# Seven block products for the output projection of the last token chunk, in a hand-scheduled two-block transformer kernel

## The chip, the cores and the metric

One core of one Trainium2 chip runs the whole program as one launch. The metric is device time in microseconds (us) of that launch. Times are quoted as the median of several runs. One further execution is recorded by the profiler; the durations in this document come from such recorded executions.

## The reference

The input x has 2048 tokens of 512 features. Two pairs of blocks follow each other, both pairs with the same weights:

```
x = x + attention(layernorm(x)) @ wo      # linear attention, 32 heads of 16 features
x = x + relu(layernorm(x) @ w1) @ w2      # hidden width 1376
```

The attention is linear: phi(t) = (t+1 if t>0 else exp(t)) + 1e-6 is applied to q and k, kv = sum over tokens of phi(k) v, and the output of a token is phi(q) kv / (phi(q) sum phi(k)). Everything is bf16 at the outside.

## The kernel before

The tokens are cut in 16 tiles of 128 and in four chunks t = 0..3 of four tiles. The code counts four layers: 0 and 2 are attentions, 1 and 3 are feed-forward layers. A name such as `2.fin12_0` is operation `fin12_0` of layer 2.

**An attention layer** makes, chunk by chunk, k and q (phi is a linear part and an exponential on ScalarE, ACT, and a minimum and maximum on VectorE, DVE), then the sum over all tokens (products `g`), and from it, in the short stage written in `bar`, a 512x512 matrix Mf: `g` is evacuated to GT (`gev`), `kv` products follow, a mask makes KVT (`kvmask`), products `m0` to `m3` with wo give Mf, evacuated one block at a time (`mev0` to `mev3`). The denominators go another way: `den` products, a logarithm and an exponential on ACT (`lnd`, `rdc`), a spreading DMA from SyncE's queue (SP, `spread`), and a DVE product that scales q (`pqs`).

The **output projection** of a tile i is then `fin`: four matmuls of 128x128 by 128x512 into one PSUM bank (for tiles 0 to 3 two calls, `fin0_0` with the first two blocks of Mf and `fin0_2` with the others). `resid` on DVE adds the bank to the residual stream xres and sums the rows, `sq` on ACT sums the squares, and for every two tiles a row of small instructions on GpSimd (POOL) and DVE (`nmean`, `msq`, `var`, `veps`, `rstd`, `nbias`) leads to the normalised tiles (`norm`) and to one DMA transpose per two tiles on SP's queue (`tr0_0`, `tr0_1`, ...), which fills Tb, the operand of the next layer.

**A feed-forward layer** computes with seven block products in place of eight (`b_h7`, `b_out`): the operands are cut in 2x2 blocks, sums of blocks are formed on DVE (`hs1` to `hs4`, `ssum`), the products `h1` to `h7` of the hidden layer run in three column groups (`_0`, `_2` of two blocks, `_4` of one), each a PE call of four or two matmuls of 256 columns. Bank BA receives h1, is copied by ACT to a second bank (`hv1`, the seed, line 700), and then goes on accumulating h6, h7 and h4; h2 is added to the copy. `hr` is the ragged rest of the hidden width.

**The order of the work** is set by a list scheduler at build time (`_list_schedule`, line 471 on). Every call of `g.add` makes one operation; its priority is its place in the order of these calls plus a whole number from the table HINTS (line 422). WINDOW is 1 for every engine, so that each engine takes its operations strictly in order of priority and waits for the next one when its inputs are not there. A second kind of hint, with "!" at the end of the key, fixes which of several engines an operation runs on (line 457). All operations that have a choice have such a hint. So the order on each engine can be read from the order of the calls and the table.

Lines that matter below: 838 `warm_fill` (eight small matmuls on zeros, `fill0`), 882 `ln_norm`, 900 the DMA transposes, 930 on `phi`, 953 all matmuls, 960 `resid`, 968 `sq`, 1147 and 1148 `gev`, 1159 `kvmask`, 1166 and 1167 `mev`, 1215 and 1217 `lnd` and `rdc`, 1227 `spread`, 1235 `pqs`, 1402 `hs`, 1797 `p2`, which chooses between `a_fin_chunk` and `f7` by the table F7 (line 650).

Of the kernel before, what the change touches and what calls it, by code (L numbers as in the profile page):

```python
# [62 lines left out]
HINTS = {"0.aqsum1": -43, "0.aqsum1!": 0, "0.aqsum2": -24, "0.aqsum2!": 0, "0.aqsum3": -126, "0.aqsum3!": 0, "0.aqsum4": 36,  # L63
         "0.aqsum4!": 0, "0.as1": -10, "0.as1_2": -24, "0.as1_2!": 0, "0.as1_3": -56, "0.as1_3!": 0, "0.as2_2": -15,
         "0.as2_2!": 0, "0.as2_3": -45, "0.as2_3!": 0, "0.as3": -6, "0.as3_2": -14, "0.as3_2!": 0, "0.as3_3": -40,
         "0.as3_3!": 0, "0.as4_2": -7, "0.as4_2!": 0, "0.as4_3": -36, "0.as4_3!": 0, "0.as_h1": -9, "0.as_h2": -6,
         "0.as_id": 2, "0.bnag0": -2, "0.bnag1": -4, "0.bnag10": 33, "0.bnag11": 32, "0.bnag12": 12, "0.bnag13": 9,
         "0.bnag14": 6, "0.bnag15": -17, "0.bnag2": 5, "0.bnag3": 0, "0.bnag4": 24, "0.bnag5": 34, "0.bnag6": 0,
         "0.bnag7": -3, "0.bnag8": 41, "0.bnag9": 38, "0.bnst0": -4, "0.bnst1": -6, "0.bnst10": 13, "0.bnst11": 19,
         "0.bnst12": 7, "0.bnst13": 1, "0.bnst14": -3, "0.bnst15": -24, "0.bnst2": 1, "0.bnst3": -4, "0.bnst4": 16,  # L70
         "0.bnst5": 28, "0.bnst6": -3, "0.bnst7": -10, "0.bnst8": 35, "0.bnst9": 30, "0.den0": 9, "0.den1": 25,
         "0.den2": 16, "0.den3": -26, "0.fill0": 5, "0.fin0_0": -2, "0.fin0_2": 10, "0.fin10_0": -88, "0.fin11_0":
         -98, "0.fin12_0": -144, "0.fin13_0": -159, "0.fin14_0": -164, "0.fin15_0": -157, "0.fin1_0": -8, "0.fin1_2":
         4, "0.fin2_0": 5, "0.fin2_2": 0, "0.fin3_0": 2, "0.fin3_2": -5, "0.fin4_0": -8, "0.fin5_0": -28, "0.fin6_0":
         -19, "0.fin7_0": -36, "0.fin8_0": -91, "0.fin9_0": -89, "0.fnorm0": 2, "0.fnorm0!": 0, "0.fnorm1": -2,
         "0.fnorm1!": 0, "0.fnorm10": 44, "0.fnorm10!": 0, "0.fnorm11": 40, "0.fnorm11!": 0, "0.fnorm12": 18,
         "0.fnorm12!": 0, "0.fnorm13": 21, "0.fnorm13!": 0, "0.fnorm14": 13, "0.fnorm14!": 0, "0.fnorm15": 10,
         "0.fnorm15!": 0, "0.fnorm2": 12, "0.fnorm2!": 0, "0.fnorm3": 6, "0.fnorm3!": 0, "0.fnorm4": 35, "0.fnorm4!":
         0, "0.fnorm5": 58, "0.fnorm5!": 0, "0.fnorm6": 7, "0.fnorm6!": 0, "0.fnorm7": 10, "0.fnorm7!": 0, "0.fnorm8":
         51, "0.fnorm8!": 0, "0.fnorm9": 48, "0.fnorm9!": 0, "0.g0_0_0": 56, "0.g0_0_1": 22, "0.g0_0_2": 5,  # L80
         "0.g0_0_3": -32, "0.g0_1_0": 62, "0.g0_1_1": 24, "0.g0_1_2": 12, "0.g0_1_3": -30, "0.g0_2_0": 98, "0.g0_2_1":
         76, "0.g0_2_2": 25, "0.g0_2_3": -23, "0.g0_3_0": 54, "0.g0_3_1": 29, "0.g0_3_2": -11, "0.g0_3_3": -10,
         "0.g1_0_0": -13, "0.g1_0_1": -8, "0.g1_0_2": -6, "0.g1_0_3": -2, "0.g1_1_0": -4, "0.g1_1_1": -1, "0.g1_1_2":
         1, "0.g1_1_3": 2, "0.g1_2_0": -74, "0.g1_2_1": -4, "0.g1_2_2": -1, "0.g1_2_3": 0, "0.gev0_0": -27,
         "0.gev0_0!": 0, "0.gev0_2": -20, "0.gev0_2!": 1, "0.gev1_0": 0, "0.gev1_0!": 0, "0.gev1_2": 2, "0.gev1_2!":
         0, "0.gevz": -7, "0.gevz!": 0, "0.k0_exp": -56, "0.k0_lin": -45, "0.k10_exp": -25, "0.k10_lin": -28,
         "0.k11_em": -17, "0.k11_exp": -35, "0.k11_lin": -23, "0.k11_phi": 25, "0.k12_em": -7, "0.k12_exp": -15,
         "0.k12_lin": -4, "0.k12_phi": 1, "0.k13_em": -20, "0.k13_exp": -30, "0.k13_lin": -15, "0.k13_phi": -11,
         "0.k14_em": -40, "0.k14_exp": -52, "0.k14_lin": -54, "0.k14_phi": -29, "0.k15_em": -47, "0.k15_exp": -51,
         "0.k15_lin": -47, "0.k15_phi": -25, "0.k1_em": 56, "0.k1_exp": -47, "0.k1_lin": -36, "0.k1_phi": 117,  # L90
         "0.k2_exp": -42, "0.k2_lin": -36, "0.k3_em": 41, "0.k3_exp": -21, "0.k3_lin": -5, "0.k3_phi": 91, "0.k4_exp":
         -31, "0.k4_lin": -45, "0.k5_em": 49, "0.k5_exp": 1, "0.k5_lin": 8, "0.k5_phi": 61, "0.k6_exp": -31,
         "0.k6_lin": -25, "0.k7_em": -13, "0.k7_exp": -45, "0.k7_lin": -23, "0.k7_phi": 57, "0.k8_exp": -6,
         "0.k8_lin": 2, "0.k9_em": 28, "0.k9_exp": 20, "0.k9_lin": 16, "0.k9_phi": 42, "0.kproj0_0": -59,
         "0.kproj0_1": -57, "0.kproj10": -43, "0.kproj11": -53, "0.kproj12": -33, "0.kproj13": -43, "0.kproj14": -69,
         "0.kproj15": -67, "0.kproj1_0": -58, "0.kproj1_1": -54, "0.kproj2": -49, "0.kproj3": -30, "0.kproj4": -51,
         "0.kproj5": -7, "0.kproj6": -44, "0.kproj7": -58, "0.kproj8": -29, "0.kproj9": -20, "0.kv0_0": -24,
         "0.kv0_1": -17, "0.kv0_2": -16, "0.kv0_3": -15, "0.kv1_0": 2, "0.kv1_1": 2, "0.kv1_2": 5, "0.kv1_3": 5,
         "0.kvmask0": -18, "0.kvmask1": 6, "0.ld_w1": 35, "0.ld_w2a": 39, "0.ld_w2b": 160, "0.ld_wka": 4, "0.ld_wkb":
         4, "0.ld_wo": 34, "0.ld_wqa": 8, "0.ld_wqb": 10, "0.ld_wv0": 23, "0.ld_wvl": 29, "0.ld_x0": 2, "0.ld_x1": 2,  # L100
         "0.ld_x12": 12, "0.ld_x2": 7, "0.ld_x4": 10, "0.ld_x8": 14, "0.lnd0": 11, "0.lnd1": 35, "0.lnd2": 19,
         "0.lnd3": -24, "0.lnv0": -2, "0.lnv1": -3, "0.lnv12": 7, "0.lnv2": 8, "0.lnv3": 2, "0.lnv6": -1, "0.lnv8":
         36, "0.m0": -14, "0.m1": -8, "0.m2": 7, "0.m3": 7, "0.mev0": -9, "0.mev0!": 1, "0.mev1": -4, "0.mev1!": 1,
         "0.mev2": 9, "0.mev2!": 0, "0.mev3": 11, "0.mev3!": 0, "0.ms_hr": 1, "0.ms_nbexp": -8, "0.ms_nhalf": 1,
         "0.ms_ones": 0, "0.ms_wrm": -13, "0.msq0": 16, "0.msq10": -63, "0.msq12": -98, "0.msq14": -110, "0.msq2": 16,
         "0.msq4": 9, "0.msq6": 16, "0.msq8": -53, "0.nbias0": 34, "0.nbias0!": 0, "0.nbias10": -7, "0.nbias10!": 1,
         "0.nbias12": -57, "0.nbias12!": 0, "0.nbias14": -37, "0.nbias14!": 1, "0.nbias2": 32, "0.nbias2!": 0,
         "0.nbias4": 26, "0.nbias4!": 1, "0.nbias6": 39, "0.nbias6!": 1, "0.nbias8": 5, "0.nbias8!": 1, "0.nmean0":
         14, "0.nmean10": -64, "0.nmean12": -100, "0.nmean14": -124, "0.nmean2": 10, "0.nmean4": 7, "0.nmean6": 12,
         "0.nmean8": -54, "0.norm0": 38, "0.norm0!": 1, "0.norm1": 34, "0.norm1!": 1, "0.norm10": 62, "0.norm10!": 1,  # L110
         "0.norm11": 63, "0.norm12": 36, "0.norm12!": 1, "0.norm13": 1, "0.norm13!": 1, "0.norm14": 7, "0.norm14!": 1,
         "0.norm15": -38, "0.norm2": 34, "0.norm2!": 1, "0.norm3": 36, "0.norm4": 30, "0.norm4!": 1, "0.norm5": 35,
         "0.norm5!": 1, "0.norm6": 43, "0.norm6!": 1, "0.norm7": 38, "0.norm8": 12, "0.norm8!": 0, "0.norm9": 13,
         "0.norm9!": 0, "0.onec0": 10, "0.onec12": 49, "0.onec4": 53, "0.onec8": 76, "0.pqs0_0": -16, "0.pqs0_2": -13,
         "0.pqs1_0": -22, "0.pqs1_2": -33, "0.pqs2_0": -34, "0.pqs2_2": -55, "0.pqs3_0": 19, "0.pqs3_2": 6,
         "0.q0_0_exp": 19, "0.q0_0_lin": 1, "0.q0_1_em": 72, "0.q0_1_exp": -43, "0.q0_1_lin": -19, "0.q0_1_phi": 154,
         "0.q0_2_exp": 2, "0.q0_2_lin": -19, "0.q0_3_em": 66, "0.q0_3_exp": -46, "0.q0_3_lin": -47, "0.q0_3_phi": 126,
         "0.q1_0_exp": -18, "0.q1_0_lin": -3, "0.q1_1_em": 70, "0.q1_1_exp": -11, "0.q1_1_lin": -29, "0.q1_1_phi": 83,
         "0.q1_2_exp": 71, "0.q1_2_lin": 69, "0.q1_3_em": 92, "0.q1_3_exp": -46, "0.q1_3_lin": -32, "0.q1_3_phi": 111,
         "0.q7_2_1": -43, "0.q7_2_2": -18, "0.q7_2_3": -20, "0.q7_2_4": 43, "0.q7_2_5": -45, "0.q7_2_6": -21,  # L120
         "0.q7_2_7": -12, "0.q7_3_1": -67, "0.q7_3_2": -45, "0.q7_3_3": -41, "0.q7_3_4": -12, "0.q7_3_5": -53,
         "0.q7_3_6": -53, "0.q7_3_7": -32, "0.qc7_2_11_exp": 6, "0.qc7_2_11_lin": 10, "0.qc7_2_12_add": -12,
# [1852 lines left out]
```

## Time and profile before

| what | us |
|---|---|
| median of 3 runs | 263.33 (263.28 to 263.78) |
| the profiled execution, its own time | 262.21 |
| its span, first to last instruction | 260.5 |
| PE busy in the span | 255.3 |
| DVE busy | 230.7 |
| ACT busy | 207.5 |
| POOL busy | 60.0 |

The span is 1.71 us shorter than the execution's own time, and that execution is 1.12 us below the median. PE is TensorE's matmul row, PEld its weight loads. Matmuls overlap in the pipe: one record is longer than the distance to the next one, so the pace is read from a group of n matmuls as (its length less one record) divided by n-1.

### The profile page before, as it was taken

What the parts mean: (1) busy time and instruction counts of PE and PEld (TensorE: products, weight loads), DVE (VectorE), ACT (ScalarE), POOL (GpSimd) and SP (SyncE); (2) the same over time, 40 slices, a digit from 0 to 9 for tenths busy, and PEclk for the clock granted to TensorE, in tenths of its full rate; (3) what the DMA queues carried; (4) which work ended last, traced back from release to release, by engine and by line L of the source; (5) the groups of instructions that cost most, each with busy time, mean ns of one, the idle gap of its engine ahead of it and who ended that gap; (6) DMA issues with size and microseconds to landing.
All of it is one profiled execution on the core that took longest, in us unless ns stands there. A gap on an engine that the chain in (4) does not pass through costs nothing.

```text
span 260.5 us, 5888 instructions
## 1 busy us (share of the span) xinstructions
PE 255.3 (98%) x2176; PEld 198.9 (76%) x2176; DVE 230.7 (89%) x574; ACT 207.5 (80%) x446; POOL 60.0 (23%) x160
## 2 busy tenths in 40 slices
PE   7999999999999999999999999999999999999995
PEld 3555577834778898889888878774488988988884
DVE  4999998799989999999999899759999997876874
ACT  4999999579989988998899799786999946882200
POOL 4110000028745007240330340002875000000000
PEclk9999999999999999999999999999999999999999
DMA  7767951744351430434031030057442514200104
GB/s 206 277 148 140 330 189 21 183 101 97 68 67 32 87 58 12 91 42 63 0 60 25 0 73 11 3 113 172 95 80 50 82 23 128 56 20 3 81 3 161
DMA packets 45980, 22.46 MB, mean 86 GB/s; under 512 B 35872, under 2 KB 44416, under 8 KB 45952
## 3 DMA queue, kind: packets, MB, share of 16 engines
q1 hardware_dynamic: 45680, 21.83, 35.8%
q8 instruction: 17, 0.28, 0.4%
q10 hardware_dynamic: 272, 0.26, 0.4%
q14 instruction: 11, 0.09, 0.1%
HBM read 7.14 MB, written 2.10 MB: 35 GB/s over the span
## 4 chain that ended last, share of the span: by engine, by line
PE 85%; ACT 5%; DVE 4%; DMA 4%; SPq 1%; issue 1%
PE ps L953 84%; DVE xres L960 2%; DMA Tb<-xn 2%; SPq L1227 1%; ACT sqscr L968 1%; DMA big<-rdc 1%; DMA xin<-in_A_x_dram 1%; ACT xn L895 1%; DVE bst L847 1%; PE ps L914 0%; ACT rdc L1217 0%; DVE big L1235 0%; ACT escr L935 0%; ACT ps L700 0%; ACT lnd L1215 0%
## 5 line engine op out<-in xcount | busy, mean ns | idle before, releaser
L953 PE MATMUL ps<-w,big 128*128 128x256 bf16 (+1 forms) x256 | 32.3, 273 | 0.0
L968 ACT ACTIVATE sqscr<-xres 128x512 bf16<-128x512 f32 x48 | 29.8, 622 | 3.2 <-DVE xres L1623 1.6
L953 PE MATMUL ps<-big,xn 128*128 128x256 bf16 (+1 forms) x224 | 32.1, 288 | 0.0
L700 ACT ACTIVATE ps<-ps 128x512 f32<-128x512 f32 (+1 forms) x41 | 23.1, 573 | 10.5 <-PE ps L953 10.2
L953 PE MATMUL ps<-Mf,big 128*128 128x512 bf16 x128 | 28.6, 380 | 0.0
L953 PEld LDWEIGHTS ps<-w,big 128*128 128x128 bf16 (+1 forms) x256 | 25.0, 98 | 3.1
L953 PEld LDWEIGHTS ps<-big,xn 128*128 128x128 f16 x224 | 21.4, 98 | 6.3 <-issue 1.1
L953 PE MATMUL ps<-Tb,w 128*128 128x256 f16 x160 | 24.3, 273 | 0.0
L1436 DVE TENSOR_TENSOR big<-ps,escr 128x512 bf16<-128x512 f32 (+1 forms) x38 | 22.7, 601 | 1.3 <-ACT escr L1455 0.6
L953 PEld LDWEIGHTS ps<-Mf,big 128*128 128x128 bf16 x128 | 12.2, 98 | 14.5 <-ACT Mf L1166 0.5
L953 PE MATMUL ps<-xn,w 128*128 128x256 f16 x160 | 23.0, 273 | 0.0
L953 PE MATMUL ps<-xn,xin 128*128 128x256 f16 x160 | 22.7, 273 | 0.0
L953 PE MATMUL ps<-wqkv,Tb 128*128 128x512 bf16 (+1 forms) x96 | 20.3, 344 | 0.2 <-ACT Tb L920 0.2
L895 ACT ACTIVATE xn<-xres,nbias,rstd 128x512 f16<-128x512 f32 x24 | 19.1, 813 | 1.4 <-POOL nbias L879 1.4
L1455 ACT ACTIVATE escr<-ps 128x512 f32<-128x512 f32 (+1 forms) x38 | 18.7, 535 | 1.8 <-PE ps L953 1.8
L877 POOL TENSOR_TENSOR rstd<-veps,nhalf 128x2 f32<-128x2 f32 x24 | 18.2, 759 | 7.0 <-DVE veps L875 5.5
L869 POOL TENSOR_SCALAR mean<-s 128x2 f32<-128x2 f32 x24 | 7.2, 301 | 54.4 <-DVE xres L960 52.8
L1424 ACT ACTIVATE big<-ps 128x512 bf16<-128x512 f32 (+1 forms) x38 | 18.9, 527 | 0.4 <-PE ps L953 0.3
L953 PE MATMUL ps<-w,Tb 128*128 128x96 bf16 (+2 forms) x176 | 17.3, 225 | 0.6 <-DMA Tb<-xn 0.6
L953 PEld LDWEIGHTS ps<-Tb,w 128*128 128x128 bf16 x160 | 15.5, 98 | 2.3 <-DVE w L1384 0.2
L1445 ACT ACTIVATE big<-big 128x1024 bf16<-128x1024 bf16 (+1 forms) x16 | 14.3, 904 | 3.5 <-DVE big L1436 3.3
L953 PEld LDWEIGHTS ps<-xn,w 128*128 128x128 bf16 x160 | 15.5, 98 | 1.9 <-DVE xn L1402 0.2
(146 smaller groups left out, 639.6 us busy)
## 6 DMA issues: line engine op xcount, KB each, us to landing
big<-rdc SPq DMA_DIRECT2D x32, 128.0 KB, 2.7
xin<-in_A_x_dram SPq DMA_DIRECT2D x3, 512.0 KB, 7.0
w<-in_B_w_dram SPq DMA_DIRECT2D x1, 1376.0 KB, 7.0
w<-in_B_w_dram SPq DMA_DIRECT2D x1, 1280.0 KB, 10.1
wqkv<-in_A_wqkv_dram SPq DMA_DIRECT2D x3, 256.0 KB, 4.6
wqkv<-in_A_wqkv_dram SPq DMA_DIRECT2D x1, 512.0 KB, 4.5
wo<-in_A_wo_dram SPq DMA_DIRECT2D x1, 512.0 KB, 4.2
out_dram<-GT SPq DMA_DIRECT2D x1, 512.0 KB, 2.6
```

Source lines behind the costliest of these rows:

```text
L700: g.add(ACT, lambda e: e.activation(psv[:, b, 0:w], psv[:, src, 0:w], ACTF.Identity), [("ps", src)], [("ps", b)], C_ACT_PSUM if w == 512 e ...
L847: g.add(DVE, lambda e: e.bn_stats(bst[:, i, :], xin[:, i, :]), [("xin", i)] + list(after), [("bst", i)], C_DVE_BNST, name="bnst%d" % i)
L869: g.add(POOL, lambda e: e.tensor_scalar(mean[:, sl], s1[:, sl], -INV_D, None, ALU.mult), [("s1", i) for i in tl], [("mean", i) for i in tl ...
L877: g.add(POOL, lambda e: e.tensor_tensor(rstd[:, sl], veps[:, sl], nhalf[:, 0:n], ALU.pow), [("veps", lo), ("nhalf",)], [("rstd", i) for i ...
L895: (ACT, lambda e: e.activation(xn[:, i, :], src, ACTF.Identity, scale=rstd[:, i:i + 1], bias=nbias[:, i:i + 1]), C_ACT_SB_AP)],
L953: last = e.matmul(o, l, r, start=st, stop=sp, skip_group_check=skip)
L960: g.add(DVE, lambda e: e.scalar_tensor_tensor(xres[:, i, :], psv[:, b, :], 0.0, src, ALU.add, ALU.add, accum_out=s1[:, i:i + 1]), [("ps", ...
L968: g.add(ACT, lambda e: e.activation(sqscr[:, q, :], xres[:, i, :], ACTF.Square, scale=math.sqrt(INV_D), accum_out=s2[:, i:i + 1]), xr(i), ...
L1424: g.add_flex([(ACT, lambda e: e.activation(ap, src(), ACTF.Relu), C_ACT_PSUM if w == 512 else 270.0), (DVE, lambda e: e.tensor_scalar(ap, ...
L1436: g.add(DVE, lambda e: e.tensor_tensor(ap, sh(psv[:, bank, 0:w]), sh(other()), ALU.add), [("ps", bank)] + okeys + ([] if first else bk), q ...
L1445: g.add_flex([(ACT, lambda e: e.activation(row, row, ACTF.Relu), 945.0 if len(cs) == 2 else C_ACT_SB), (DVE, lambda e: e.tensor_scalar(row ...
L1455: g.add(ACT, lambda e, w=w: e.activation(q[:, 0:w], psv[:, bank, 0:w], ACTF.Identity), [("ps", bank)], key, C_ACT_PSUM if len(cs) == 2 els ...
```

## The change

Three things change.

1. F7 names chunk 3 for layer 2, so that the last chunk of the second attention goes through `f7` in place of `a_fin_chunk`. Four 512-column calls of 128x512 matmuls (`fin12_0` to `fin15_0`, 16 matmuls) give way to seven calls of four matmuls of 256 columns (`f7_3_1` to `f7_3_7`). DVE forms four sums of blocks of Mf (`fwsum1` to `fwsum4`, into GT) and four of the scaled q (`fsum1_3` to `fsum4_3`). ACT copies one bank (`fv1_3`). The four `resid` become two `fm` (512 columns) and eight `fc` (256 columns, with row sums), and two small additions on POOL (`s1add12`, `s1add14`) join the row sums of the halves.
2. `ln_norm` has a third choice, POOL, for tiles whose normalisation had DVE and ACT to choose from.
3. The HINTS table is another one: 972 priorities and 35 engine choices of operations that both kernels have differ.

```diff
-        F7 = {0: (), 2: ()}
+        F7 = {0: (), 2: (3,)}
...
             g.add_flex([(DVE, ts[1], 460.0),
-                        (ACT, lambda e: e.activation(xn[:, i, :], src, ACTF.Identity, scale=rstd[:, i:i + 1], bias=nbias[:, i:i + 1]), C_ACT_SB_AP)],
+                        (ACT, lambda e: e.activation(xn[:, i, :], src, ACTF.Identity, scale=rstd[:, i:i + 1], bias=nbias[:, i:i + 1]), C_ACT_SB_AP), ts],
```

The function that is now called, shortened (it stands in both kernels):

```python
def f7(t, first_layer):
    ...
    a11, a12, a21, a22 = bigv[:, 4:6, t, lo], bigv[:, 6:8, t, lo], bigv[:, 4:6, t, hi], bigv[:, 6:8, t, hi]
    ...
    def prod(n, bank, X, W, opens, reads):
        def mk():
            return [(psv[:, bank, 256 * p:256 * p + 256], X[:, d, 128 * p:128 * p + 128], W[:, d, :], opens and p == 0 and d == 0, d == 1, True)
                    for p in range(2) for d in range(2)]
        mm_group(mk, list(reads) + mk_, [("ps", bank)], 4 * C_MM256, "f7_%d_%d" % (t, n))
    prod(1, BA, a11, b11, True, k1)
    BB = seed(BA, 512, "fv1_%d" % t)
    prod(5, BC, sb_[0], tw[0], True, sk[0] + gk[0])
    prod(6, BA, sb_[1], tw[1], False, sk[1] + gk[1])
    mid("m5", BC, f1, 1)
    prod(2, BB, a12, b21, False, k2)
    mid("m6", BA, f0, 1)
    fin("c11", BB, f0, 0)
    prod(7, BA, sb_[2], tw[2], False, sk[2] + gk[2])
    prod(3, BC, sb_[3], b22, False, sk[3])
    fin("c22", BA, f1, 1)
    fin("c12", BC, f0, 1)
    ...
    prod(4, BA, a22, tw[3], False, k2 + gk[3])
    fin("c21", BA, f1, 0)
```

Hints that the text below speaks of, old and new. A dash means that the kernel has no such operation.

```
0.fill0        5 ->  80     0.ld_w2b  160 ->  41     0.mev0!   DVE -> ACT
2.fin10_0   -153 -> -144    2.fin11_0 -149 -> -153   2.fin14_0 -166 -> -
2.f7_3_5       - -> -63     2.f7_3_1    - -> -46     2.f7_3_4     - -> -24
3.h1_0_0      39 ->  22     3.h1_0_2   26 ->   2     3.h5_1_4    35 ->   7
3.h7_1_0      32 ->  34     2.gev1_2! DVE -> ACT     2.mev2!   DVE -> ACT
2.norm8!     DVE -> POOL    2.norm10! ACT -> POOL    2.norm12! ACT -> POOL
2.norm13!    DVE -> POOL    2.norm14! DVE -> ACT
```

The order of PE's calls around the change, read from the calls and the two tables:

```
before: kv1_0 kv1_1 kv1_2 kv1_3 fin1_0 fin2_0 m2 m3 fin0_0 fin3_0 fin1_2 fin0_2 fin3_2 fin2_2 fin5 fin4 fin6 fin7
        fin9 fin8 fin10 fin11 fin15 fin12 fin13 fin14 | h1_0_0 h1_0_2 hr0 h5_0_4 h2_0_0 h5_0_0 h5_0_2 h6_0_0 ...
after:  g1_2_3 kv1_0 m1 kv1_1 kv1_2 kv1_3 m0 den3 m3 m2 fin0_0 fin1_0 fin1_2 fin0_2 fin2_0 fin3_0 fin3_2 fin2_2 fin4
        fin5 fin6 fin7 fin8 fin9 fin11 fin10 | h1_0_2 h1_0_0 h2_0_2 hr0 h5_0_0 h5_0_2 h6_0_0 h5_0_4 ... h5_1_4
        f7_3_5 h7_1_0 h4_0_4 h3_1_2 h7_1_2 f7_3_1 h4_1_0 h1_1_4 f7_3_3 h3_1_4 f7_3_6 ... f7_3_2 p1_0 f7_3_7 ... f7_3_4
```

2 lines of the change are left out of this document (1 added, 1 removed), and 579 rows, old and new, of the table HINTS.

## The prediction

> **What bounds the kernel now.** I read the page's totals first, then the waits of PE, then the chain that ended last in order of time.
>
> ```profile
> PE 255.3 (98%) x2176; PEld 198.9 (76%) x2176; DVE 230.7 (89%) x574; ACT 207.5 (80%) x446; POOL 60.0 (23%) x160
> ```
> ```profile
> PE ps L953 <- DMA Tb<-xn: 0.6, 1, 0.6
> ```
> ```profile
> 47.58 0.53 ACT rdc L1217
> ...
> 51.80 2.67 DMA big<-rdc
> ...
> 70.18 4.40 DMA Tb<-xn
> ...
> 74.71 183.07 PE ps L953 x1674
> ```
>
> PE is busy 98% of the span, and after the head it waits once, 0.6 us at 74.71, for a DMA transpose of the first attention. From there the chain is 183 us of matmuls end to end. So three things count: less work on PE, a gap on PE that closes, a gap that opens. A faster or slower DVE, ACT or POOL counts only through such a gap. Whether "busy" is also full pace is seen in two stretches of PE's timeline, one of 512-column matmuls (the output projection) and one of 256-column ones:
>
> ```profile
> 177.16 13.11 PE L953 MATMUL ps<-Mf,big 128*128 128x512 bf16 x60
> 190.11 1.04 PE L953 MATMUL ps<-Tb,w 128*128 128x256 f16 x8
> ...
> 192.32 1.91 PE L953 MATMUL ps<-xn,xin 128*128 128x256 f16 x16
> ```
> ```profile
> L953 PE MATMUL ps<-Mf,big 128*128 128x512 bf16 x128 | 28.6, 380 | 0.0
> L953 PE MATMUL ps<-w,big 128*128 128x256 bf16 x240 | 31.4, 273 | 0.0
> ```
>
> The pace is (13.11 - 0.38)/59 = 0.2158 us for 512 columns and (1.91 - 0.27)/15 = 0.1093 us for 256. Both stretches have no hole in them.
>
> **The work on PE.** Sixteen matmuls of 0.2158 us go, 3.45 us. Twenty-eight of 0.1093 us come, 3.06 us. PE has 0.39 us less to do: **-0.39**. No row shows the block products of the projection themselves; the same shape at the same pace (0.1093) stands in every feed-forward row, weight loads included, so I take that.
>
> Here the Trainium skill, "TensorE: Matmul & The Clock Gate", section Back-to-back issue gap, speaks against the change: for streams of weight load and matmul it gives about 81 ns at 128 columns and 131 ns at 512. By an estimate halfway between (about 98 ns at 256), the sixteen would take 2.1 us and the twenty-eight 2.7 us, +0.6. The trace does not agree: 0.2158 us at 512 columns. It agrees with that section's other formula, columns/2.4 + 2.5 ns, which gives 216 and 109 ns.
>
> **The head.** `fill0` moves from behind the first transpose to a place ahead of the projection of tile 4, and two halves of q products move forward into the two small holes.
>
> ```profile
> 5.42 0.62 PE L842 MATMUL ps<-wrm 128*128 128x128 bf16 x8
> ...
> 6.28 1.47 PE L953 MATMUL ps<-wqkv,Tb 128*128 128x512 bf16 x6
> ...
> 8.78 0.72 PE L914 MATMUL ps<-ident,xn 128*128 128x128 f16 x8 [0.16 <-DVE xn L885]
> 9.34 0.38 PE L953 MATMUL ps<-Tb,wqkv 128*128 128x256 f16 x2
> 9.91 1.04 PE L953 MATMUL ps<-wqkv,Tb 128*128 128x512 bf16 x4 [0.19 <-ACT Tb L920]
> ```
>
> Without the fill, the first projection still starts at 6.28, because it waits for ACT's copy of tile 0. Two halves of 2 x 0.109 = 0.22 us fill the holes ahead of 8.78 and 9.91 (about 0.33 us each in issue time), 0.44 us gained; the fill, at (0.62 - 0.22)/7 = 0.057 us a matmul, costs 0.45 us later. **0.0**, between -0.1 and +0.45 (holes not filled).
>
> **The wait at 74.71.** It ends a chain that runs through `rdc1` (47.58), SP's spreads, the `pqs` products and a DVE without a pause to the transposes.
>
> ```profile
> 46.08 0.61 SPq L804 DMA_DIRECT2D w<-in_B_w_dram  x1
> ```
> ```profile
> 46.99 0.59 ACT L1066 ACTIVATE big<-ps 128x512 bf16<-128x512 f32 x1
> 47.47 0.63 ACT L1217 ACTIVATE rdc<-lnd 128x512 bf16<-128x512 f32 x1
> ```
> ```profile
> 49.15 0.68 DVE L1167 CAST Mf<-ps 128x512 bf16<-128x512 f32 x1
> ```
>
> By the new table the last load (0.61 us on SP's queue) goes ahead of the spreads, `rdc1` goes ahead of the linear part that it followed (0.48 us), and `mev0` leaves DVE for ACT (0.6 us). The next spreads then start when SP has issued the two of `rdc2`, 0.3 us earlier than before. I take **-0.3**. Bounds: -0.64 (the wait is all there is to win) and +0.2 (other orders in that stage changed too).
>
> **The bar of layer 2.** The new order puts `m0` late, `m3` and `m2` right ahead of the first `fin`, and only two half `fin` between `m2` and `fin1_2`. All work ahead of the fins ends at 177.16 less the four half-fin matmuls done early (0.86), so `fin0_0` is due at 176.30.
>
> ```profile
> 175.08 0.40 PE L953 MATMUL ps<-big,Zc 128*32 128x512 bf16 x4
> 175.41 0.62 PE L953 MATMUL ps<-GT,wqkv 128*128 128x128 bf16 x8
> 175.87 1.03 PE L953 MATMUL ps<-Mf,big 128*128 128x512 bf16 x4
> 176.73 0.60 PE L953 MATMUL ps<-wo,KVT 128*128 128x512 bf16 x2
> ```
> ```profile
> 51.19 0.38 ACT L1147 ACTIVATE GT<-ps 128x256 bf16<-128x256 f32 x1 [0.71 <-PE ps L953]
> ...
> 177.37 0.60 ACT L1166 ACTIVATE Mf<-ps 128x512 bf16<-128x512 f32 x1 [1.58 <-PE ps L953]
> ```
>
> Counted back from 176.30: `m3` and `m2` 0.43, `den3` 0.42 with its change of mode, `m0` 0.22, `kv1_3` and `kv1_2` 0.11 each, so that `kv1_2` is due at 175.01. Ahead of it stand `kv1_1`, `m1` and `kv1_0` (0.44), so the last issue of `g1_2_3` is at 174.46 and its record ends at 174.73; its evacuation takes ACT 0.38 and some 0.04 on each side, until 175.17: 0.16 us late. Then `m3` and `m2` start at 176.04 and 176.26. ACT evacuates both, 0.49 us apart, and the second ends at about 177.55, while `fin0_0` and `fin1_0` (0.43 each) have ended at 177.33: 0.24 us. **+0.40**, between 0 (the order covers it) and +0.8.
>
> **The hand-over to the last layer.** Before, PE reached the first `h1` at 190.11, behind sixteen fins that now stand later. It gets there at 190.11 - 3.45 + 0.40 = 187.06, and tiles 0 and 1 must then have been transposed.
>
> ```profile
> 178.66 0.69 DVE L960 SCALAR_TENSOR_TENSOR xres<-ps,xres 128x512 f32<-128x512 f32 x1
> 179.28 0.08 DVE L960 DVE_READ_ACCUMULATOR xres<-ps,xres 128x1 f32 x1
> ```
> ```profile
> 182.46 0.71 POOL L877 TENSOR_TENSOR rstd<-veps,nhalf 128x2 f32<-128x2 f32 x1
> ```
> ```profile
> 184.28 1.50 ACT L895 ACTIVATE xn<-xres,nbias,rstd 128x512 f16<-128x512 f32 x2
> ...
> 190.78 1.05 ACT L700 ACTIVATE ps<-ps 128x512 f32<-128x512 f32 x2
> ```
> ```profile
> 185.81 2.62 SPq L900 DMA_TRANSPOSE Tb<-xn  x2
> ```
> ```profile
> Tb<-xn SPq DMA_TRANSPOSE x29, 3.2
> ```
>
> Before, the first `resid` began at 178.66 and the transpose was issued at 185.81. Now only two half fins precede `fin1_2`: it ends at 178.17 and `resid1` begins at 178.2, behind `fwsum1` and `fwsum2`, which still fit. On POOL `rstd0` comes straight behind `veps0`, without a `nmean2` ahead of it. What sets the rest is order: `nbias0` stands on DVE behind three more `resid` and a `pqs` (each 0.61 apart), until 182.0, and `norm0` on ACT behind `sq3` and `sq2`. So the two norms run from 182.1 to 183.5, the transpose is issued at about 183.65 and lands, 3.2 later, at 186.85, 0.2 ahead of PE. SP issues the second one 1.3 later, landing at 188.2. But the new order has only `h1_0_0` (0.44) between `h1_0_2` and `h2_0_2`, which waits for the copy of its bank by ACT (0.6 from the record's end at 187.66): 188.3 against 187.93. **+0.37**, between 0 and +1.0 (transposes 0.6 late).
>
> **The other engines beyond.** What the change adds to DVE, from the nearest rows (the same shapes in other layers), and where there is room:
>
> ```profile
> L1402 DVE TENSOR_TENSOR xn<-Tb 128x512 f16<-128x512 f16 x16 | 6.7, 422 | 0.9 <-DMA Tb<-xn 0.7
> L1602 DVE TENSOR_TENSOR xres<-ps,xres 128x512 f32<-128x512 f32 x15 | 10.1, 687 | 1.6 <-PE ps L953 1.5
> L1623 DVE SCALAR_TENSOR_TENSOR xres<-ps,xres 128x256 f32<-128x256 f32 x32 | 12.6, 420 | 2.2 <-PE ps L953 2.2
> L890 DVE TENSOR_SCALAR xn<-xres,mean,rstd 128x512 f16<-128x512 f32 x12 | 6.4, 544 | 0.0
> ```
> ```profile
> 200.00:210.00 10.00, 10.00 (x104) 8.99 (x102) 9.21 (x20) 9.97 (x21) 1.30 (x3) 1.00 0.42 68
> 210.00:220.00 10.00, 10.00 (x93) 8.82 (x92) 8.37 (x17) 4.74 (x9) 0.00 (x0) 1.00 0.16 58
> ```
>
> Eight sums (3.4), two `fm` (1.4), eight `fc` with their accumulator reads (4.0), less four `resid` (3.1): +5.7 us. Three norms (0.544 each) and two casts (0.68, and about 0.4 for the one half as wide) leave DVE, -2.7. The remaining 3 us fall between 187 and 215, where the moved `resid` alone vacate 3.1 before 192 and DVE idles 0.8 and 1.6 us in the two stretches above. ACT gains a copy and loses two norms for one; POOL, at 1.30 of 10 us there, takes four norms. DVE keeps pace, so I put **0**; without that cover PE waits for a bank by one DVE instruction, up to +0.7. Chunk 3's transposes stood behind the first stores on SP, long after its old norms, and still do:
>
> ```profile
> 218.58 2.64 SPq L900 DMA_TRANSPOSE Tb<-xn  x2
> ```
>
> **Sum.** -0.39 + 0.0 - 0.3 + 0.40 + 0.37 + 0 = **+0.08** on a span of 260.5 and an execution of 262.21. That execution lies 1.12 below the median of the runs, 263.33; carried over, **263.4**.
>
> **The rivals.**
>
> *The hand-over is covered.* If the two waits of the bar and the wait for the bank copy don't appear (each rests on 0.2 to 0.4 us of estimated latency), and the wait at 74.71 shrinks by 0.3 to 0.64, what stays is -0.39 - 0.3 to -0.39 - 0.64: 262.6 to 262.3. For it speaks that PE had no gap anywhere from 74.71 on; against it that each wait follows from the new order and old durations. 0.22.
>
> *PE reaches the last layer before its operand* (the slower side). Its place is the first `h1`, its price one for one. It decides when the first transpose is issued later than 183.9. With the old distance from `resid` to the issue (185.81 - 178.66 = 7.15) it would be issued at 178.2 + 7.15 = 185.35 and land at 188.55, 1.5 late: 263.33 - 0.39 - 0.3 + 0.40 + 1.5 = 264.5, or 264.9 with the bank copy too. For it speaks the chain above, whose slack is 0.2 us; against it the freer POOL and ACT. 0.27.
>
> *The seven products save PE nothing.* If 512-column matmuls ran in 0.131 us, as no group here does while 256 stayed at 0.109, sixteen would cost 2.1 us, twenty-eight 3.06, the -0.39 would turn to +0.96 and the time to 264.8. 0.02.
>
> **How the numbers follow.** This kernel's measurement can tell about 0.2%, 0.53 us, from no change: 262.80 to 263.86. The forecast (0.49) runs from 262.9 to 263.9, nearly all within that. Slower holds the second and third rivals, 0.29; faster the first, 0.22; the forecast's own edges cancel. The range leaves a tenth on each side: 262.5 to 264.5.
>
> **What would show it.** PE's timeline: seven groups of four 256-column matmuls reading big and Mf or GT, 0.44 us each, between 199 and 211. PE's waits: the wait for the DMA at 74 shorter or gone; new ones near 175.2, 177.5 and 188, of 0.15 to 0.4 us, for ACT. SP's timeline: the first transpose of layer 2 near 183.7. PE's `fin` group shorter by sixteen. Wrong would be: PE waiting for Tb near 187, or for DVE between 195 and 215, or no wait at all.

## The result, and the profile after

The changed kernel takes 263.81 us (median of 12 runs, 263.54 to 265.95), the kernel before 262.56 us beside it (12 runs, 261.96 to 263.78): ratio 1.0055, 95% interval 1.0038 to 1.0072. Run again on another occasion, it took 263.82 against 262.37 us, ratio 1.0067 (1.0040 to 1.0094). So the change costs 1.25 to 1.45 us. The forecast was 263.4 us, "within 0.2%", with the change itself at +0.08. That the time lies inside the range is luck in part. Two errors of opposite sign nearly cancel: the change cost some 1.3 us more than the sum said, and the base of three runs (263.33) stood 0.8 us above the median of the twelve that include them.

The page's totals of the kernel after, and its waits of PE:

```profile
span 262.5 us, 5909 instructions
...
PE 254.8 (97%) x2177; PEld 199.7 (76%) x2188; DVE 231.1 (88%) x585; ACT 211.5 (81%) x452; POOL 65.7 (25%) x164
```
```profile
PE ps L956 <- DMA Tb<-xn: 1.2, 1, 1.2
...
PE ps L956 <- DMA wqkv<-in_A_wqkv_dram: 0.5, 1, 0.5
PE ps L956 <- ACT ps L703: 0.2, 1, 0.2
```

(Lines of kernel.py moved by three: L953 is now L956.) PE is still the bound. The one wait behind the head, 0.6 us before, is now 1.2, and two others have come, 0.5 us for a load of weights and 0.2 us for ACT. PE's timeline, start, duration, group, and the idle time ahead of it:

```profile
10.49 0.39 PE L956 MATMUL ps<-Tb,wqkv 128*128 128x256 f16 x2 [0.54 <-DMA wqkv<-in_A_wqkv_dram]
...
75.98 0.84 PE L956 MATMUL ps<-w,Tb 128*128 128x96 bf16 x16 [1.19 <-DMA Tb<-xn]
...
175.92 1.04 PE L956 MATMUL ps<-GT,wqkv 128*128 128x128 bf16 x8
176.79 0.38 PE L956 MATMUL ps<-wo,KVT 128*128 128x512 bf16 x1
177.10 0.40 PE L956 MATMUL ps<-big,Zc 128*32 128x512 bf16 x4
177.48 0.60 PE L956 MATMUL ps<-wo,KVT 128*128 128x512 bf16 x2
177.92 10.95 PE L956 MATMUL ps<-Mf,big 128*128 128x512 bf16 x47
188.70 1.04 PE L956 MATMUL ps<-Tb,w 128*128 128x256 f16 x8
189.98 0.61 PE L956 MATMUL ps<-Tb,w 128*128 128x256 f16 x4 [0.24 <-ACT ps L703]
...
202.05 0.60 PE L956 MATMUL ps<-GT,big 128*128 128x256 bf16 x4
...
258.57 1.40 PE L956 MATMUL ps<-xin,big 128*128 128x256 bf16 x10
```

And the last group of the kernel before, which the prediction did not look at:

```profile
256.52 1.25 PE L953 MATMUL ps<-xin,big 128*128 128x256 bf16 x10
```

Four rows cut an execution into parts that can be compared between kernels: the matmul behind the wait near 74 (A ends), the first `h1` of the last layer (B ends), the end of PE's last group (C ends), and the execution's time (D).

| profiled execution | A | B | C | D | sum |
|---|---|---|---|---|---|
| before | 74.71 | 115.40 | 67.66 | 4.44 | 262.21 |
| after | 75.98 | 112.72 | 71.27 | 4.57 | 264.54 |

B lost 3.45 us of fins and should have fallen to 111.95: it is 0.77 too long. C got 28 matmuls, 3.06 us, and grew by 3.61: 0.55 too long. D is 0.13 longer. A is 1.27 longer in this execution. B, C and D hardly differ between executions of one order (B of the four other profiles below that keep after's layer 2 lies at 112.52, 112.54, 112.59 and 112.94, C at 71.27 each time); A does, by a microsecond, since it hangs on when the first loads arrive: in the five profiles with before's order of layers 0 and 1 throughout (before, e2, e8, e11, e12), DVE waits 2.6, 2.4, 3.1, 3.7 and 3.1 us in all for tiles of x, and A is 74.71, 74.61, 75.35, 75.58 and 75.20. Taken from the medians instead, with B + C + D at 188.42 after (B 112.59, the median of the five) and 187.50 before, A is 263.81 - 188.42 = 75.4 against 262.56 - 187.50 = 75.1. So about 0.9 us of the loss stands in layers 2 and 3, and 0.3 (0.5 on the second occasion) in the first two layers, in a part of the trace in which nothing of the seven products is computed.

### The profile page after: what moved, and what is told of

It reads as the page before. It is cut to its first block, busy times and chain, and to the rows that moved or that the text cites. A ratio compares the mean times of both kernels' runs of the same rounds, so it can differ in the third digit from the quotient of the medians.

```text
span 262.5 us, 5909 instructions
## 1 busy us (share of the span) xinstructions
PE 254.8 (97%) x2177; PEld 199.7 (76%) x2188; DVE 231.1 (88%) x585; ACT 211.5 (81%) x452; POOL 65.7 (25%) x164
## 4 chain that ended last, share of the span: by engine, by line
PE 79%; ACT 6%; DMA 5%; DVE 5%; SPq 2%; issue 1%; POOL 0%; POOLq 0%
PE ps L956 78%; DVE xres L963 3%; DMA wqkv<-in_A_wqkv_dram 3%; ACT sqscr L971 2%; DMA Tb<-xn 2%; SPq L1230 1%; DVE big L1238 1%; DMA big<-rdc 1%; ACT xn L898 1%; ACT lnd L1218 1%; ACT ps L703 1%; SPq L766 1%; ACT rdc L1220 0%; ACT Mf L1169 0%; SPq L771 0%
## 5 line engine op out<-in xcount | busy, mean ns | idle before, releaser
L956 PE MATMUL ps<-w,big 128*128 128x256 bf16 (+1 forms) x256 | 32.8, 272 | 0.0
L956 PE MATMUL ps<-big,xn 128*128 128x256 bf16 (+1 forms) x221 | 31.3, 287 | 0.2
L956 PEld LDWEIGHTS ps<-w,big 128*128 128x128 bf16 (+1 forms) x256 | 25.0, 98 | 3.0
L956 PE MATMUL ps<-Mf,big 128*128 128x512 bf16 (+1 forms) x121 | 26.8, 369 | 0.4 <-issue 0.2
L956 PEld LDWEIGHTS ps<-big,xn 128*128 128x128 f16 x224 | 21.4, 98 | 5.7 <-issue 0.7
L956 PE MATMUL ps<-Tb,w 128*128 128x256 f16 x160 | 24.2, 273 | 0.2 <-ACT ps L703 0.2
L956 PE MATMUL ps<-xn,w 128*128 128x256 f16 x160 | 23.5, 273 | 0.0
L1458 ACT ACTIVATE escr<-ps 128x512 f32<-128x512 f32 (+1 forms) x38 | 19.3, 547 | 4.9 <-PE ps L956 4.9
L956 PE MATMUL ps<-xn,xin 128*128 128x256 f16 x160 | 23.2, 272 | 0.0
L956 PEld LDWEIGHTS ps<-Mf,big 128*128 128x128 bf16 x124 | 11.7, 98 | 13.6 <-ACT Mf L1169 1.1
L880 POOL TENSOR_TENSOR rstd<-veps,nhalf 128x2 f32<-128x2 f32 x24 | 19.1, 795 | 10.4 <-DVE veps L878 8.9
L1427 ACT ACTIVATE big<-ps 128x512 bf16<-128x512 f32 (+1 forms) x39 | 20.3, 538 | 0.3 <-PE ps L956 0.2
L956 PE MATMUL ps<-wqkv,Tb 128*128 128x512 bf16 (+1 forms) x93 | 19.8, 342 | 0.2
L898 ACT ACTIVATE xn<-xres,nbias,rstd 128x512 f16<-128x512 f32 x23 | 18.3, 818 | 1.5 <-POOL nbias L882 1.4
L956 PE MATMUL ps<-w,Tb 128*128 128x96 bf16 (+2 forms) x176 | 17.2, 224 | 1.2 <-DMA Tb<-xn 1.2
L956 PEld LDWEIGHTS ps<-Tb,w 128*128 128x128 bf16 x160 | 15.4, 98 | 2.8 <-ACT ps L703 0.5
L936 ACT ACTIVATE big<-ps 128x512 bf16<-128x512 f32 x24 | 17.0, 792 | 0.5 <-PE ps L956 0.5
L956 PEld LDWEIGHTS ps<-xn,w 128*128 128x128 bf16 x160 | 15.5, 98 | 2.0 <-DVE xn L1405 0.2
## 6 DMA issues: line engine op xcount, KB each, us to landing
wqkv<-in_A_wqkv_dram SPq DMA_DIRECT2D x3, 256.0 KB, 4.6
```

What stands on the lines that cost most here:

```text
L880: g.add(POOL, lambda e: e.tensor_tensor(rstd[:, sl], veps[:, sl], nhalf[:, 0:n], ALU.pow), [("veps", lo), ("nhalf",)], [("rstd", i) for i ...
L898: (ACT, lambda e: e.activation(xn[:, i, :], src, ACTF.Identity, scale=rstd[:, i:i + 1], bias=nbias[:, i:i + 1]), C_ACT_SB_AP), ts],
L936: ops = [g.add(ACT, lambda e: e.activation(dst_ap, psv[:, b, :], ACTF.Identity, bias=1.0 + 1e-6, scale=1.0), [("ps", b)], [dst_key], C_ACT ...
L956: last = e.matmul(o, l, r, start=st, stop=sp, skip_group_check=skip)
L1427: g.add_flex([(ACT, lambda e: e.activation(ap, src(), ACTF.Relu), C_ACT_PSUM if w == 512 else 270.0), (DVE, lambda e: e.tensor_scalar(ap, ...
L1458: g.add(ACT, lambda e, w=w: e.activation(q[:, 0:w], psv[:, bank, 0:w], ACTF.Identity), [("ps", bank)], key, C_ACT_PSUM if len(cs) == 2 els ...
```

## The experiments

**First set: which layers lose.** The time lies at separate places (theory A), or all in the change proper (rival B). The order of the first two layers is swapped alone, in both directions, and one pair of matmuls in the head alone.

```diff
 # e1_front_new: the kernel before, every hint of layers 0 and 1 as after
-"0.aqsum2": -24, ... "1.wsum5": -38
+"0.aqsum2": -16, ... "1.wsum5": -37
 # e2_back_new: the kernel after, every hint of layers 0 and 1 as before
```

> The kernel before with the new kernel's order for layers 0 and 1 alone; layers 2 and 3 as before, no block products in the output projection. Theory A (the time is lost at separate places, most of it in the first two layers, where PE's timeline of the kernel after had fallen 0.7 us behind by 45 us and 1.27 us behind the wait for the DMA transpose at 74): +0.7 to +1.3 us against before, PE with a wait of about 0.5 us for a load of wqkv near 10 us and one of about 1.2 us for Tb near 75. Rival B (the offset of the first two layers belongs to that one execution, the change proper costs all of the time): -0.2 to +0.3 us.

Measured: 263.66 against 262.23 us, ratio 1.0050 (1.0025 to 1.0074), +1.4. In its profile A is 76.27, B 115.40 and C 67.65: everything lost in A, with a wait of 1.37 us for Tb near 75 and none for wqkv.

> The kernel after with the order of before for layers 0 and 1; layers 2 and 3, the seven products and the choice of engines as in after. Theory A: the rest of the loss, 0.77 (bar of layer 2) + 0.24 (bank copy) + 0.3 (unplaced) - 0.39 (less work on PE) = +0.9 by one profile, so +0.1 to +0.9 us against before; PE's waits as in before up to 74.7. Rival B: +1.2 us or more. Rival C (the change proper gains, as my covered rival said): -0.2 to -0.6 us.

Measured: 263.49 against 262.23 us, ratio 1.0047 (1.0028 to 1.0067), +1.3. A 74.61, B 112.94, C 71.27, D 4.56: by the profile +1.27 in B, C and D, nothing in A. That is above theory A's range and in rival B's, and this profile's B is the longest of the five. Rival C (a gain) is out, and B as a single cause is out too, since the first experiment loses as much without any of the products. The two losses don't add up to 2.7 in the kernel after, which has both. With the same order of layers 0 and 1, A from the medians is 76.2 in the first experiment (263.66 - 187.50) and 75.4 in after. Why is not shown; A is the part that varies.

```diff
 # e3_qh_early: the kernel before          # e4_qh_late: the kernel after
-"0.qh0_0_0_1": -6                         -"0.qh0_0_0_1": -42
+"0.qh0_0_0_1": -42                        +"0.qh0_0_0_1": -6
```

> The kernel before with one pair of q matmuls alone moved, from the 27th place on PE's list of operations to ahead of the projection of tile 2, where after has it. Theory A: it waits for the load of the second half of the q weights, 0.3 to 0.6 us near 10 us, and everything behind it on PE is late by that: +0.3 to +0.6 us. Rival D (the wait at 74.71 for the DMA has 0.64 us to swallow it): the wait near 10 is there, the one at 74 is shorter by the same, the time +-0.15 us.

Measured: 262.31 against 262.23 us, ratio 1.0000 (0.9978 to 1.0021). In its profile PE doesn't wait for wqkv at all. Nor does it in the profiles of e1, e5 and e6, which have the pair forward too (0.33 us in e9): the 0.54 us of the profile of after belong to an execution whose loads were late. Moved forward, the pair costs nothing that shows, with 0.6 us as the bound.

> The kernel after with that one pair of q matmuls put back to its old place, all else as in after. Theory A: no wait for wqkv near 10 us, time 0.3 to 0.6 us below after (so +0.7 to +1.1 against before). Rival D: the wait at 74 grows by what the head gains, time as after (+1.2 to +1.5 against before).

Measured: 265.89 against 262.23 us, ratio 1.0133 (1.0097 to 1.0170; four runs), 2 us above the kernel after, which neither theory allows. PE's timeline of its head shows why:

```profile
5.09 1.23 PE L920 MATMUL ps<-ident,xn 128*128 128x128 f16 x8 [0.26 <-DVE xn L891]
6.39 2.74 PE L959 MATMUL ps<-wqkv,Tb 128*128 128x512 bf16 x6
8.92 1.06 PE L959 MATMUL ps<-Tb,wqkv 128*128 128x256 f16 x4
```

Six 512-column matmuls take from 6.39 to 8.92, 0.42 us each instead of 0.216: PE runs at half pace, as it does in the warm-up block at the kernel's start (3.6 us for eight), and goes on so until about 10. The column of the granted clock reads 1.00 all the while, but it takes a stretch for which the trace holds no clock record as 1.00. The first record, at full clock, starts at 10.03 us here, and between 4.30 and 6.17 us in the ten profiles with full pace there that have one. So this run doesn't tell what the pair costs. Like the kernel after, it has no `fill0` between the transposes at 5 us. That gave a new theory, F: the fill keeps PE busy while its pace is still open.

**Second set: the fill.** The kernel after once more, and the fill moved alone in both kernels.

```diff
 # e6_fill_early: the kernel after         # e7_fill_late: the kernel before
-"0.fill0": 80                             -"0.fill0": 5
+"0.fill0": 5                              +"0.fill0": 80
```

> The kernel after, unchanged, beside the next three on the same chip. Theory F (fill0, moved behind the first projections, no longer keeps PE busy ahead of them; in some executions they then run at half pace, as in the profile of the run before this one, where 512-column matmuls near 7 us took 0.43 us each): +1.2 to +2 us against before, with single executions another 1 to 2 us above the others. Rival G (the head is the same in every execution but for the arrival of the loads): +1.2 to +1.6 us and a spread like that of before.

Measured: 263.82 against 262.37 us, six runs from 263.55 to 265.30. The slowest was the profiled one, and it shows the half pace in the unchanged kernel after (the first clock record starts at 10.24 us):

```profile
5.07 1.23 PE L920 MATMUL ps<-ident,xn 128*128 128x128 f16 x8 [0.24 <-DVE xn L891]
6.37 2.74 PE L959 MATMUL ps<-wqkv,Tb 128*128 128x512 bf16 x6
8.90 1.06 PE L959 MATMUL ps<-Tb,wqkv 128*128 128x256 f16 x4
```

> The kernel after with fill0 alone put back behind the first transpose. Theory F: the first projections run at 0.216 us a 512-column matmul in every execution; the time is 0.3 to 1 us below the kernel after, and no execution stands 1 us above the others. Rival G: within 0.3 us of the kernel after, or 0.3 above it, since the fill costs its 0.45 us on PE at either place.

Measured: 263.89 against 262.37 us, ratio 1.0064 (1.0041 to 1.0087); six runs from 263.57 to 264.57. The row that starts the projections:

```profile
6.35 1.47 PE L959 MATMUL ps<-wqkv,Tb 128*128 128x512 bf16 x6
```

Full pace, and no run above 264.6; but the median is that of after, so rival G holds for the median. Whether single executions at half pace are gone, as F said, six runs can't tell.

> The kernel before with fill0 alone moved to where after has it. Theory F: +0.3 to +2 us against before, most of it in the first 12 us of PE's timeline, where the 512-column matmuls take 0.43 instead of 0.216 us. Rival G: -0.2 to +0.3 us.

Measured: 262.92 against 262.37 us, ratio 1.0019 (1.0001 to 1.0036). The fill moved alone costs 0.5 us (0.03 to 0.94) in the kernel before, inside F's range; its profiled execution ran at full pace and was no slower (A 74.54).

The Trainium skill, "TensorE: Matmul & The Clock Gate", section What's actually happening, says that the array starts at half clock and is released after a window of about 3.4 us that was busy enough, and that these windows run free of the kernel. The halves agree (0.42 and 0.216 us), and so does it that one kernel shows both kinds of head. Steps of that length show in the clock records too: one at 0.50 (in e8, below) lasts 3.41 us, and those at 1.00 that end inside a trace last 10.24, 252.6, 256.0 or 259.4, whole multiples of it. That it is decided by how busy a window was is the page's explanation; no run here tests it.

**A repair that failed.** If the waits of B and C are of order alone, the order of before should take them away.

```diff
 # e8_repaired: e2's kernel, and
+ layer 2 up to fin3, resid3 and its spreads: hints of before ("2.mev2!" and "2.gev1_2!": DVE)
+ "2.fwsum1": -19, "2.fwsum2": -13
+ "3.h2_0_2": 22
+ products, sums and stores of the last chunk: hints of before
```

> The seven products as in after; layers 0 and 1 in the order of before; in layer 2 the order and the engines of before up to the output projection (both m2's copy and gev1_2 back on DVE), with the sums of the products behind the first resid; h2_0_2 three groups later; the last chunk and its stores in the order of before. Theory A (bar 0.77, bank copy 0.41 and tail 0.15 us are waits of order, not of work): all three gone, -0.2 to -0.6 us against before. Rival H (the waits come from the added products' sums on DVE or from fins arriving earlier): +0.2 to +0.8 us.

Measured: 270.84 against 262.37 us, ratio 1.0320 (1.0287 to 1.0352). Two things in PE's timeline:

```profile
178.48 6.49 PE L959 MATMUL ps<-Mf,big 128*128 128x512 bf16 x28
185.68 3.63 PE L959 MATMUL ps<-Mf,big 128*128 128x512 bf16 x16 [0.71 <-DVE big L1241]
190.56 1.05 PE L959 MATMUL ps<-Tb,w 128*128 128x256 f16 x8 [1.26 <-DMA Tb<-xn]
...
257.62 1.25 PE L959 MATMUL ps<-w,big 128*128 128x256 bf16 x5 [2.65 <-DVE xres L1605]
258.66 0.42 PE L959 MATMUL ps<-w,Tb 96*128 96x256 bf16 x1
...
262.05 0.71 PE L959 MATMUL ps<-w,big 128*128 128x256 bf16 x5
```

The 2.65 us at the end are my own doing, since I had mixed two orders of the last chunk. The hole cost more than itself: inside it, at 257.5, the granted clock falls to 0.50, and it stays there until 260.9. Five matmuls of 256 columns take 1.25 us behind it and 0.71 later; sixteen at some 0.21 us instead of 0.109 make 1.7 us. With the hole that is what C (75.59) is longer than after's (71.27), 4.3 us. And B says something: at 115.21, only 0.2 of the 3.45 us of removed fins was gained. With before's order PE waits 0.71 us for DVE's scaled products and 1.26 us for the transposes of tiles 0 and 1. That is the second rival of the prediction, absent in the kernel after: its new order of the bar pays 0.6 to 1.0 us in B, mostly at the bar, and doesn't pay more at the hand-over.

**Third set: the terms one by one.**

```diff
 # e9_front_fill: e1's kernel with "0.fill0": 5
 # e10_chain74: the kernel before, and only
-"0.ld_w2b": 160, "0.rdc1": 41, "0.qc7_3_21_lin": 7, "0.mev0!": DVE, ...
+"0.ld_w2b": 41, "0.rdc1": 38, "0.qc7_3_21_lin": 11, "0.mev0!": ACT, ... (mev1, spread0 to spread2 as after)
```

> The kernel before with the new order of layers 0 and 1 (as in the first experiment), but fill0 at its old place. Theory F: no execution with half-pace projections is left, so the time falls from that experiment's +1.3 to +0.2 to +0.7 us against before; what is left is the longer wait for the transposes near 75. Rival I (the new order of the first attention costs it all, the fill nothing): +1.0 to +1.5 us. My prediction's own terms for this part (head 0.0, wait at 74.71 -0.3) would give -0.3 us.

Measured: 262.99 against 262.25 us, ratio 1.0028 (1.0005 to 1.0052): +0.7, theory F's upper end, and 0.7 below the first experiment, from which only the fill's place differs. The wait near 75 is 1.03 us in its profile.

> The kernel before with only the three edits of the first attention's end that my term for the wait at 74.71 was built on: the last weight load ahead of the spreads on SP, rdc1 ahead of the linear part on ACT, mev0 from DVE to ACT (and the new order of the spreads). By that term: the wait at 74.71 is 0.1 to 0.6 us, the time -0.5 to 0 us. Rival J (the spreads wait behind the load's transfer or DVE's order does not follow): the wait is 0.9 to 1.4 us, the time +0.2 to +0.7 us.

Measured: 262.15 against 262.25 us, ratio 1.0001 (0.9975 to 1.0026). That is -0.66 to +0.68 us, so the run tells neither the forecast (-0.5 to 0) from nothing nor the two from a small loss. The wait is 0.50 us. The view puts it down to ACT's copy, but the transpose, issued at 70.6, took 4.2 us and so landed some 0.1 us ahead of PE's start at 74.87, as it did before (74.58 and 74.71). SP's queue tells what became of the 0.3 us in three profiles. Each row is one issue of a spread: the first of all, the one that waits for `rdc1`, the longest, and the last of those that the DVE products (`pqs`) and then the `resid` wait for. First the kernel before, then after, then this one:

```profile
43.43 0.66 SPq L1227 DMA_DIRECT2D big<-rdc  x1
...
48.12 0.54 SPq L1227 DMA_DIRECT2D big<-rdc  x1
...
50.00 1.11 SPq L1227 DMA_DIRECT2D big<-rdc  x1
...
51.80 0.60 SPq L1227 DMA_DIRECT2D big<-rdc  x1
```
```profile
44.11 0.66 SPq L1230 DMA_DIRECT2D big<-rdc  x1
...
48.54 0.61 SPq L1230 DMA_DIRECT2D big<-rdc  x1
...
50.50 1.41 SPq L1230 DMA_DIRECT2D big<-rdc  x1
...
52.60 0.60 SPq L1230 DMA_DIRECT2D big<-rdc  x1
```
```profile
43.81 0.66 SPq L1229 DMA_DIRECT2D big<-rdc  x1
...
48.24 0.61 SPq L1229 DMA_DIRECT2D big<-rdc  x1
...
50.20 1.35 SPq L1229 DMA_DIRECT2D big<-rdc  x1
...
52.24 0.60 SPq L1229 DMA_DIRECT2D big<-rdc  x1
```

From the first spread to the one behind `rdc1` it was 4.69 us before and is 4.43 in both others: the 0.3 us are there. But the long issue takes 1.41 and 1.35 us for 1.11, and to the last spread it is 8.37 before, 8.49 after and 8.43 here. That the new order lengthens this issue is not shown. Over all profiles it takes 1.09 to 1.46 us in the seven with before's order of the spreads and 0.85 to 2.06 in the seven with the new one: between executions it varies by more than the 0.3 us that were to be won.

```diff
 # e11_bank_tail: e2's kernel, and
+ "3.h2_0_2": 22; products, sums (of chunk 3 and the last of chunk 2) and stores at the end as before
 # e12_best: e11's kernel, and
+ "2.mev2!": DVE, "2.fwsum1": -18, "2.fwsum2": -13, "2.fin2_0": 1
```

> The second experiment's kernel (layers 0 and 1 of before, the rest of after) with h2_0_2 three groups later and the last chunk's products, sums and stores in the order of before. Theory A (bank copy 0.41 us and last bank 0.15 us are waits of order, and the end after PE's last matmul another 0.12): 0.4 to 0.7 us below the second experiment, +0.5 to +0.9 us against before, no PE wait for ACT near 189, the last ten matmuls in 1.25 us. Rival K (another bank or operand is late in their place): +1.0 to +1.4 us.

Measured: 263.63 against 262.25 us, ratio 1.0051 (1.0030 to 1.0072), no better than e2's 263.49. Rival K. Where `h2_0_2` waited for the bank stands another wait, for the transposes, and the last group is back at its length while D grew from 4.56 to 4.81:

```profile
189.67 0.85 PE L959 MATMUL ps<-w,Tb 128*128 128x96 bf16 x16 [0.17 <-DMA Tb<-xn]
...
258.26 1.25 PE L959 MATMUL ps<-xin,big 128*128 128x256 bf16 x10
```

> The kernel of the run before this one, and in layer 2 m2's copy back on DVE behind pqs1_0, the sums of the product weights behind resid0, and fin2_0 ahead of fin1_2. Theory A: of the bar's 0.77 us the part behind the first fins (0.4) goes, and PE still finds its operand at the last layer: 0.2 to 0.5 us below that run, +0.1 to +0.6 us against before. Rival L (the hand-over has only about 0.2 us of slack, so what the bar gives back is lost in a wait for Tb at the first h1): within 0.2 us of that run, with a PE wait for the DMA of Tb near 188.

Measured: 264.24 against 262.25 us, ratio 1.0069 (1.0046 to 1.0092). Neither fits: the median is 0.6 us above that run (the intervals overlap), where rival L said within 0.2. The wait of 0.26 us behind the first fins is gone, but more was lost behind it, 0.69 us in the fins for DVE's scaled products and 0.16 at the hand-over; B is 113.47 for 112.88.

```profile
185.17 3.63 PE L959 MATMUL ps<-Mf,big 128*128 128x512 bf16 x16 [0.69 <-DVE big L1241]
...
189.88 0.85 PE L959 MATMUL ps<-w,Tb 128*128 128x96 bf16 x16 [0.16 <-DMA Tb<-xn]
```

No version with the products came below the kernel before.

## Why the prediction was right or wrong, step by step

**The work on PE, -0.39: right.** Seven groups of four stand between 202.05 and 211.46, as forecast; C grows by 3.06 us and the waits named below, B falls by 3.45 and its own. The rival in which the products save nothing is out.

**The head, 0.0 (to +0.45): mis-sized.** The step took the fill as 0.45 us of work that goes from one place to another, hidden by two filled holes. Moved alone it cost 0.5 us, the bound, and put back in e1's kernel it won 0.7 (e9). What I missed is what it may be there for: without it some executions run the first projections at half pace (seen in two of the five profiles without it and in none of the nine with it; in the one of after 265.3 instead of about 263.7 us). That this moves the median of the kernel after is not shown: put back there, it left 263.89 for 263.82. At full pace the head costs nothing that shows: the first spread is issued at 43.34 to 44.33 with before's order and at 43.49 to 44.11 with the new one, at half pace at 45.17 and 45.30. The load that the profile shows PE waiting for was no fault of the step: alone, that move cost nothing.

**The wait at 74.71, -0.3: wrong in direction.** It grew, from 0.64 to 1.19 us in the two profiles, and it is 0.94 to 1.54 us in all six with the new order of layers 0 and 1, at most 0.74 in the eight others. The step that failed is the one that let three moved operations stand for the stage and gave the rest, "other orders in that stage changed too", at most +0.2. From the first spread to the matmul behind the wait it takes 30.62 to 31.49 us in the seven profiles with before's order of this stage, 31.06 in e10, which has only the three, and 31.50 to 32.72 in the six with the new order. Whether the three would win 0.3 by themselves stays open (e10). That the spreads "start ... 0.3 us earlier" came true (0.26), but behind them stands the long issue, whose 1.11 us the profile of before showed and the step did not look at.

Along the chain that ended last, after is longer than before by 0.12 us from the first spread to the last, by 0.25 from there to the norm that the transpose waits for, and by 0.22 from that norm to the landing. In the second piece ACT's order has changed: one `sq` now stands ahead of two bank copies, and from the start of the two norms ahead of it to this one ACT takes 4.1 to 4.3 us in all six profiles, 3.5 in the eight others (it has one `sq` less to do ahead of those two norms, so the chain loses only part of it).

```profile
66.27 1.52 ACT L898 ACTIVATE xn<-xres,nbias,rstd 128x512 f16<-128x512 f32 x2
67.70 0.61 ACT L971 ACTIVATE sqscr<-xres 128x512 bf16<-128x512 f32 x1
...
68.32 1.05 ACT L703 ACTIVATE ps<-ps 128x512 f32<-128x512 f32 x2
...
70.40 0.81 ACT L898 ACTIVATE xn<-xres,nbias,rstd 128x512 f16<-128x512 f32 x1
```

In the third, the transpose takes 4.4 to 5.0 us from issue to landing in the six and 3.5 to 4.4 in the eight; why is not shown. An `nbias` on DVE that takes 0.15 us with before's order takes 0.56 in all six, but it isn't what the norm waited for: it ended at 70.01, and ACT came to the norm at 70.40.

```profile
69.44 0.57 DVE L882 TENSOR_TENSOR nbias<-mean,rstd 128x2 f32<-128x2 f32 x1
```

**The bar, +0.40: right in kind, 0.24 too small.** B is 0.57 to 0.99 us too long, median 0.64, and both waits are where they were put. The `kv1` group takes 0.87 us from 175.92 to 176.79 for eight matmuls of some 0.055, 0.44, and for `m1`, 0.22, whose record is missing on PE in this profile (its weight load stands at 175.98) and present in the others, as in e2's:

```profile
174.93 0.38 PE L959 MATMUL ps<-wo,KVT 128*128 128x512 bf16 x1
```

So 0.21 us is lost where the step put 0.16. The fins take 10.78 us from 177.92 to 188.70 for 48 x 0.2158 = 10.36: 0.42 where it put 0.24, and 0.28 to 0.42 in the five profiles. 0.26 of that stands behind the first fins in each, as forecast. Some 0.1 of B's median is not placed. ACT has three copies in a row there and not two, since `m0` had been moved late as well, so that the last ends at 178.99.

```profile
176.12 0.39 ACT L1150 ACTIVATE GT<-ps 128x256 bf16<-128x256 f32 x1 [0.26 <-PE ps L956]
...
177.21 1.78 ACT L1169 ACTIVATE Mf<-ps 128x512 bf16<-128x512 f32 x3 [0.16 <-PE ps L956]
```

**The hand-over, +0.37: right.** The first transpose was issued at 185.30 (the forecast 183.65, with the 1.27 of A and 0.37 more at the bar, makes 185.29). It landed some 0.25 us ahead of PE at 188.70, so PE found tiles 0 and 1 ready, and `h2_0_2` waited for ACT's copy of its bank: eight matmuls from 188.70 would end their issue at 189.57, the next starts at 189.98, +0.41. Where other orders let PE come early, it waited for Tb: in e8 at the first `h1`, 1.26 us, and in e11 and e12 at the ragged product `hr0`, which needs the second transpose too, 0.17 and 0.16. So the second rival was real and lay just beyond the order chosen.

**The other engines, 0: right for 190 to 215, and blind at the end.** Behind `h2_0_2` PE waits for no bank there. But I had looked at the tail's engines and not at the order of the last products: the last ten matmuls take 0.15 us more, for a bank that DVE frees, and D is 0.13 longer.

**The sum.** In layers 2 and 3, -0.39 + 0.64 + 0.41 + 0.15 + 0.13 = +0.94. A is what the medians leave, 0.3 to 0.5, so it is no check that the two make the measured +1.25 to +1.45; by the medians of the profiles the stage ahead of the wait alone is longer by 0.8 (32.1 for 31.3). Of the 1.3 that were missing in +0.08, some 0.7 belong to A, 0.3 to the tail and 0.25 to the bar. Left open: why the long issue on SP varies between 0.85 and 2.06 us, why the transposes of the first attention land later with the new order, and whether the fill's place moves the median of the kernel after.

## What to carry to other kernels

Work taken out of the stretch that hides a chain (here sixteen fins over norm and transpose) is saved there only as far as the chain gets shorter too: 2.8 of 3.45 us with after's order of the bar, 0.2 in e8. What an order pays to start that chain sooner is the price of the change, so look for it first. When an edit lets a queue start earlier, see how much the longest single issue in that queue varies between executions before counting the gain. Where executions differ by as much as the effect, cut the trace at events all kernels share and compare part by part, and take the base from many runs.

## What the runs showed of the hardware

PE can run a kernel's first matmuls at half pace (0.42 us for 512 columns instead of 0.216) up to 10.0 and 10.2 us into it; the same kernel did so in one profiled execution and not in another. The column of the granted clock reads 1.00 there only because the trace has no clock record for that stretch. Late in e8, inside a hole of 2.65 us on PE, the granted clock fell to 0.50 and stayed there for 3.41 us. An issue of a spread on SP takes 0.60 us, but the ninth or tenth of the first twelve took 0.85 to 2.06 us over fourteen profiles, and in e9 this:

```profile
49.22 2.06 SPq L1229 DMA_DIRECT2D big<-rdc  x1
```
